# Loading k, b and v of the first three chunks in eight-step rows in a fused recurrence and feed-forward kernel

## The chip, the cores and the metric

The kernel runs on one core of one Trainium2 chip. The metric is the device time of one execution in microseconds (us), and less is better. A profile shows one execution with its engines: PE multiplies matrices and turns (transposes) tiles, with PEld its weight loads; DVE, ACT and POOL work element by element; SP issues most DMAs. PE writes to PSUM, here four slots of two banks each, and DVE and ACT read it from there.

## The reference

A recurrence over 768 steps for 4 batches of 8 heads with 40 features, and then a feed-forward layer on its output. `state` is a 40 by 40 matrix for each of the 32 heads:

```python
for t in range(S):
    y[:, :, t] = np.einsum('bhd,bhde->bhe', rt, state)
    Sa = np.einsum('bhde,bhe->bhd', state, at)
    state_decay = state * wt[:, :, None, :] - np.einsum('bhd,bhe->bhde', Sa, bt)
    state = state_decay + np.einsum('bhd,bhe->bhde', vt, kt)
...
x = attn_out.transpose(0, 2, 1, 3).reshape(B * S, H * D)      # 3072 x 320
h = x @ w_in                                                   # 320 x 2048
r = np.maximum(h, 0.0)
return ((r * r) @ w_out).astype(np.float32)                    # 2048 x 320
```

All inputs and the output are float32; the kernel multiplies in bfloat16.

## The kernel before

The 768 steps are cut into 12 chunks (`NCH`) of 64 steps. Within a chunk the recurrence is written as matrix products, and only the state goes from chunk to chunk. Partitions hold 64 steps twice: half `g` holds the 16 heads of two batches.

`load(c)` issues the DMAs of a chunk on SP. w, k, b and v are loaded "steps first": one partition for each step, and in it a run of 40 numbers (160 bytes) for each of 16 heads. a and r are loaded "in eight-step rows": eight steps of one head stand together in DRAM, so that one run has 320 numbers (1,280 bytes); partitions are then pairs of heads and groups of eight steps.

`prep(c)` makes the factors of a chunk. `ln` takes logarithms of w; `hi` and `lo` split them into two bfloat16 parts; `ci` sums them over the steps by a triangular matrix, and `ei` and `ex` take exp of minus and plus the sum (`iG`, `Gin`); `cf` makes the same sums turned, features on the partitions, and `ef` their exp (`GT`). `mulKB` (two halves) multiplies the loaded k and b by `iG` into `KB`, steps first. `TK` turns `KB` on PE and `tK` copies it to `KBT`, features first. `castA`, `TA`, `tA` and `castR`, `TR`, `tR` bring a and r features first (`AR`); `castV` copies v into one half of `VU`. The products `EN` of `KBT` and `AR` are masked by `mEN` into a triangle.

`rec(c)` is the recurrence: `AS` (state times a) and `EV` (triangle times v) add up in one PSUM slot, `u0` copies it, `NU` adds the second order term, and `u1` writes u beside v into `VU`. `SC` and `S` make the new state, `s` scales it, and `TS` and `tS` turn it. So the chain from chunk to chunk goes AS, EV, u0, NU, u1, S, s.

`read(c)` makes the output: `TV` turns the whole of `VU` and `tV` copies it to `VUT`; `CX` and `mCX` are the second triangle; `RS` and `Y` give the output, `y` and `yd` scale it, and `XT` and `xt` turn it. `ffn(c)` is the feed-forward layer of 256 rows: for each quarter `u`, `F` and `FL` multiply by the first matrix, `f` cuts at zero, `q` squares, and `O` multiplies by the second matrix; `o` copies the result out and `st` stores it.

`weights()` loads the matrices in pieces into buffers that other work uses later, and casts them: `lwl` and `cwl` (the last 64 rows of the first matrix), `lwi` and `cwi` (its four quarters of 256 rows), `lwo` and `cwo` (eight pieces of the second). The quarters use two buffers in turn, so a load of a quarter waits for the cast of the quarter two before it. Chunks 0 to 3 (`WHOLE`) are turned by 128 by 128 transposes, the later ones by narrower ones, two at a time.

The order of all this is written out in the string `ORDER`, some 1,000 entries such as `PE0 TK 0` or `POOL castV 0 g1`: an engine (for PE the PSUM slot too) and a step. Each engine runs its entries strictly in that order; the waits between engines follow from the data. SP's queue is such a list too: a DMA that waits for its buffer holds back all DMAs behind it. Every PE step is recorded at line 385 (products), 389 (narrow turns) or 392 (wide turns), and copies at 366 (DVE), 371 (ACT) and 375 (POOL), so that steps are told apart by their tiles.

## Time and profile before

| | |
|---|---|
| Median of three runs | 254.06 us |
| The runs | 254.0, 254.06 and 254.92 us |
| Profiled execution, first to last instruction (the only time that its profile gives) | 254.1 us |
| Busy: PE, DVE, ACT, POOL | 225.3, 180.6, 161.0, 150.5 us |
| Mean granted PE clock | 0.962 of full speed |
| Moved by DMA | 33.55 MB in 114,089 packets, 101,238 of them under 512 bytes |

The profiled execution is one run and its span stands within 0.1 us of the median. Busy times of different engines overlap. "Idle before" in a profile line is the time for which an engine had nothing to run ahead of that instruction, with what ended it. A PE that is busy is not always at its full clock: the column of the granted clock tells.

### The profile page before, as it was taken

The page shows a single profiled execution, that of the slowest core. Times are in us where ns is not written, and L with a number is a line of the kernel's source. Part 1 is how long each engine was busy: PE and PEld are TensorE (multiplying, and loading weights), DVE is VectorE, ACT ScalarE, POOL GpSimd, SP SyncE. Part 2 cuts the span into 40 slices and gives each one's busy share as a digit, 9 for nine tenths or more (in the row PEclk, how much of TensorE's full clock was granted, in tenths as well). Part 3 has the DMA queues.
Part 4 walks back from the last instruction along what each step waited for, and adds up shares of the span by engine and source line. Part 5 has one row for each costly group of instructions (what it writes and reads, how often), then busy time and mean ns, then how long its engine had stood idle before and what let it go on. Part 6 is the DMA issues. An engine that isn't in the chain of part 4 may idle for free.

```text
span 254.1 us, 12021 instructions
## 1 busy us (share of the span) xinstructions
PE 225.3 (89%) x5472; PEld 176.3 (69%) x5472; DVE 180.6 (71%) x216; ACT 161.0 (63%) x233; POOL 150.5 (59%) x128
## 2 busy tenths in 40 slices
PE   0547768999888999998999989999999999999991
PEld 0436757777776877776777777767777787878870
DVE  7463895987976976887659877799566779667301
ACT  3435676678955889773677657776578563762920
POOL 3581710695874688198688563998459950320860
PEclk9975697999999999999999999999999999999998
DMA  6999897888888986885586988798570020202021
GB/s 133 181 212 164 182 238 159 188 157 215 207 138 202 193 162 135 172 153 113 114 159 173 201 143 161 141 165 167 112 142 19 4 57 3 57 3 54 0 50 56
DMA packets 114089, 33.55 MB, mean 132 GB/s; under 512 B 101238, under 2 KB 113014, under 8 KB 114038
## 3 DMA queue, kind: packets, MB, share of 16 engines
q1 hardware_dynamic: 113894, 32.62, 64.1%
q8 instruction: 43, 0.70, 1.2%
q10 hardware_dynamic: 144, 0.16, 0.2%
q14 instruction: 8, 0.07, 0.1%
...
## 4 chain that ended last, share of the span: by engine, by line
PE 58%; DMA 12%; SPq 8%; ACT 7%; DVE 7%; issue 4%; POOL 3%; ACTq 0%; POOLq 0%; DVEq 0%
PE pb L385 49%; PE pb L389 5%; DMA raw_w<-in_w_dram 4%; PE pb L392 4%; SPq L411 2%; SPq L404 2%; DMA osb<-in_moe_w_out_dram 2%; POOL KB L379 2%; DVE EN L605 2%; DMA raw_r<-in_r_dram 2%; DMA raw_kb<-in_b_dram 2%; SPq L435 1%; DMA raw_kb<-in_k_dram 1%; SPq L425 1%; ACT iG L493 1%
## 5 line engine op out<-in xcount | busy, mean ns | idle before, releaser
L852 POOL TENSOR_TENSOR G<-G 128x1024 bf16<-128x1024 bf16 x37 | 69.4, 1891 | 37.5 <-ACT G L844 37.3
L385 PE MATMUL pb<-WOUT,G 128*128 128x320 bf16 x384 | 57.3, 300 | 1.0 <-ACT WOUT L371 0.9
L385 PE MATMUL pb<-XT,WIN 128*128 128x256 bf16 x384 | 48.8, 274 | 0.0
L844 ACT ACTIVATE G<-pb 128x1024 bf16<-128x1024 f32 x37 | 37.4, 1024 | 14.7 <-PE pb L385 14.6
L385 PEld LDWEIGHTS <-G 128*128 128x128 bf16 x384 | 35.4, 98 | 15.2 <-issue 1.7
L379 POOL TENSOR_TENSOR KB<-raw_kb,iG 128x640 bf16<-128x640 f32 x20 | 30.6, 1542 | 24.3 <-DMA raw_kb<-in_b_dram 14.6
L385 PEld LDWEIGHTS <-WIN 128*128 128x128 bf16 x384 | 34.7, 98 | 8.3 <-issue 3.7
L605 DVE TENSOR_TENSOR CX<-pb,MSKI 128x1024 bf16<-128x1024 f32 x24 | 29.1, 1219 | 5.2 <-PE pb L385 4.6
L605 DVE TENSOR_TENSOR EN<-pb,MSK 128x1024 bf16<-128x1024 f32 x24 | 29.0, 1221 | 4.8 <-PE pb L385 3.7
L499 ACT ACTIVATE Gin<-pb 64x320 f32<-64x320 f32 x48 | 20.3, 428 | 6.3 <-PE pb L385 5.8
L580 DVE TENSOR_TENSOR AR<-pb,GT 128x512 bf16<-128x512 bf16 x24 | 15.7, 683 | 10.1 <-PE pb L392 4.2
L697 DVE TENSOR_TENSOR STb<-pb,GT 64x640 bf16<-64x640 f32 x22 | 18.0, 819 | 5.8 <-PE pb L385 5.5
L371 ACT ACTIVATE VU<-pb 64x640 bf16<-64x640 f32 x24 | 16.7, 697 | 7.4 <-PE pb L385 7.1
L493 ACT ACTIVATE iG<-pb 128x640 f32<-128x640 f32 x24 | 16.7, 698 | 6.3 <-PE pb L385 4.7
L775 DVE TENSOR_TENSOR Yb<-pb,Gin 128x128 bf16<-128x128 f32 (+1 forms) x24 | 12.4, 550 | 11.4 <-PE pb L385 11.4
L385 PEld LDWEIGHTS <-EN 64*64 64x64 bf16 x768 | 15.0, 113 | 6.2 <-issue 3.2
L379 POOL TENSOR_TENSOR lo<-lnW,hi 128x640 bf16<-128x640 f32 x12 | 16.8, 1398 | 3.8 <-issue 3.2
L366 DVE COPY KBT<-pb 128x2048 bf16<-128x2048 bf16 x12 | 14.6, 1219 | 5.7 <-PE pb L389 3.5
L371 ACT ACTIVATE osb<-pb 128x640 f32<-128x640 f32 (+1 forms) x13 | 8.4, 644 | 15.4 <-PE pb L385 14.9
L375 POOL CAST VU<-raw_v 64x640 bf16<-64x640 f32 x20 | 15.2, 761 | 4.8 <-DMA raw_v<-in_v_dram 4.2
L846 DVE TENSOR_SCALAR G<-pb 128x1024 bf16<-128x1024 f32 x11 | 13.4, 1220 | 5.2 <-PE pb L385 4.7
L385 PE MATMUL pb<-XT,WLAST 64*128 64x256 bf16 x192 | 16.4, 271 | 0.2 <-DVE CX L605 0.2
...
## 6 DMA issues: line engine op xcount, KB each, us to landing
...
```

The source lines that it names most:

```text
L366: lambda: nc.vector.tensor_copy(out=o_(), in_=i_())))
L371: alts.append(("ACT", c_act(n), lambda: nc.scalar.activation(out=o_(), in_=i_(), func=ACTF.Copy, scale=1.0 if scale is None else scale)))
L375: lambda: nc.gpsimd.tensor_copy(out=o_(), in_=i_())))
L379: return [("POOL", 40 + 2.35 * n, lambda: nc.gpsimd.tensor_tensor(out=o_(), in0=a_(), in1=b_(), op=op)), ("DVE", c_dve(n), lambda: nc.vect ...
L385: return lambda: nc.tensor.matmul(out=o_(), lhsT=l_(), rhs=r_(), start=start, stop=stop, skip_group_check=True)
L493: ew(f"ei {c} h{jh}", [("ACT", c_act(2 * n), lambda hb=hb, jh=jh: nc.scalar.activation(out=iG[0][:].rearrange("p (g j) e -> p g (j e)", g= ...
L499: nc.scalar.activation(out=Gin[c % NGI][rows(g), NP * jh:NP * jh + NP, :].rearrange("p j e -> p (j e)"), in_=slot(hb, FP32)[rows(g), g, 0: ...
L580: ew(f"tA {c} g{g}", [("DVE", c_dve(512), lambda g=g: nc.vector.tensor_tensor(out=steps(AR[q2][:, 0, g]), in0=turned(ha, g), in1=steps(GT[ ...
L605: evac(f"m{nm} {c} g{g}", lambda s, n: [("DVE", c_dve(n), lambda: nc.vector.tensor_tensor(out=dst[q2][:, g, s].rearrange("p q i t -> p (q ...
L697: ew(f"s {c} q{q}", [("DVE", c_dve(2 * n), lambda q=q: nc.vector.tensor_tensor(out=STb[q2][rows(q), :, q, 0:D], in0=slot(hs, FP32)[rows(q) ...
L844: ("ACT", c_act(1024), lambda gb=gb, hf=hf: nc.scalar.activation(out=gb, in_=slot(hf, FP32)[:], func=ACTF.Relu)),
L852: ("POOL", 1900, lambda gv=gv: nc.gpsimd.tensor_tensor(out=gv, in0=gv, in1=gv, op=ALU.mult)),
```

## The change

Chunks 0 to 2 (`RUNS` for k and b, `VRUNS` for v) get a path of their own.

- k, b and v of these chunks are loaded in eight-step rows, runs of 1,280 bytes in place of 160.
- `turned_kb` takes the place of `ei`, `mulKB`, `TK` and `tK`. It casts k and b to bfloat16 (`castK`, `castB`), turns them (`TK`, 32 narrow transposes), multiplies by exp of minus the turned sums (`eg`, from the slot of `cf`) in `tK`, two halves, and turns the product back (`BK`, 16 wide transposes) to fill `KB` (`bK`).
- `turned_v` takes the place of `castV` and of the v half of `TV`: `castV`, 16 narrow transposes (`VT`), two copies into `VUT` (`vt`), 16 transposes back (`BV`) and two copies into `VU` (`bV`).
- `turned_u` turns the u half alone: `UT`, and two copies (`ut`).
- Each quarter of the first matrix is loaded by two DMAs with runs of 1,024 bytes in place of one with 2,048.
- There are three more small buffers (`tKB` twice, `tV`), which are cleared at the start.
- `ORDER` is new throughout, for the steps of all chunks. Its beginning, up to the first state:

```
SP ldw 0; SP ldb 0; SP ldw 1; SP ldk 0; ACT ln 0; POOL hi 0; SP ldv 0; POOL lo 0; SP lda 0; POOL
castB 0; PE0 ci 0 h1; PE1 cf 0; SP ldw 2; ACT ex 0 h1 g1; ACT ln 1; DVE castK 0; PE2 TK 0; ACT eg
0; SP ldv 1; DVE castV 0; ACT ex 0 h1 g0; PE3 VT 0; DVE tK 0 g1; ACT ef 0; PE0 ci 0 h0; POOL castA
0; SP ldk 1; ACT vt 0 g0; DVE tK 0 g0; PE1 TA 0; ACT ex 0 h0 g1; SP ldb 1; ACT hi 1; DVE tA 0 g0;
PE2 BK 0; ACT vt 0 g1; DVE tA 0 g1; SP lda 1; ACT ex 0 h0 g0; PE3 BV 0; ACT castV 1; DVE lo 1; ACT
bK 0; PE1 VT 1; SP ldr 0; POOL castK 1; PE0 cf 1; DVE vt 1 g0; ACT ef 1; DVE bV 0 g0; PE2 EN 0 g0;
SP lwl 0; DVE bV 0 g1; DVE mEN 0 g0; ACT vt 1 g1; PE3 EN 0 g1; POOL castB 1; ACT eg 1; SP ldr 1;
DVE mEN 0 g1; PE1 TK 1; ACT ln 2; POOL castA 1; PE0 ci 1 h1; SP ldb 2; PE2 ci 1 h0; DVE tK 1 g0;
PE3 EV 0; ACT ex 1 h0 g1; POOL castR 0; ACT ex 1 h0 g0; SP lda 2; ACT ex 1 h1 g0; POOL hi 2; PE2
TR 0; DVE tK 1 g1; ACT ex 1 h1 g1; ACT u0 0; POOL lo 2; PE0 TA 1; SP lwi 0 u0; ACT tR 0 g1; PE NU
0; DVE tA 1 g1; ACT cwl 0; PE1 BK 1; DVE tA 1 g0; DVE u1 0 g0; PE0 EN 1 g0; DVE tR 0 g0; ACT u1 0
g1; SP lwi 0 u1; DVE bK 1; PE2 EN 1 g1; PE3 ci 2 h1; DVE mEN 1 g1; ACT ex 2 h1 g0; PE1 UT 0; SP
ldw 3; ACT ex 2 h1 g1; ACT ut 0 g0; PE3 S 0 g0; DVE mEN 1 g0; PE2 ci 2 h0; ACT ut 0 g1; ACT ex 2
h0 g0; PE1 CX 0 g0; ACT castA 2; DVE mCX 0 g0; PE0 BV 1; ACT castR 1; PE S 0 g1; ACT bV 1 g1; DVE
s 0 q0; PE1 cf 2; SP ldk 2; ACT ex 2 h0 g1; DVE s 0 q1; ...
```

The code, without the new `ORDER`:

```diff
+    RUNS = range(3)
+    VRUNS = range(3)
...
+    tKB = buf("tKB", [128, 8, 2, 64], BF16, 2)
+    tV = buf("tV", [128, 8, 2, 64], BF16, 1)
...
+    def runs_of(c, y):
+        return raw_kb[c % NKBR][:].rearrange("p h e -> p (h e)")[:, 640 * y:640 * y + 640].rearrange(
+            "p (q x) -> p q x", q=2)
...
-        for nm, x in (("k", k), ("b", b)):
+        for y, (nm, x) in enumerate((("k", k), ("b", b))):
+            def go_runs(y=y, x=x):
+                xv = x[:, :, t0, :].rearrange("b (p q) (k i) e -> q (b p) k (i e)", q=2, i=8)
+                for q in range(2):
+                    nc.sync.dma_start(out=runs_of(c, y)[:, q, :], in_=xv[q])
+            if c in RUNS:
+                plan.add(f"ld{nm} {c}", [("SP", 1100)], ("ew", {"SP": go_runs}),
+                         writes=[("raw", nm, c % NKBR)])
+                continue
...
+        def go_v_runs():
+            xv = v[:, :, t0, :].rearrange("b (p q) (k i) e -> q (b p) k (i e)", q=2, i=8)
+            to = raw_v[c % NV][:].rearrange("p (q i) e -> p q (i e)", q=2)
+            for q in range(2):
+                nc.sync.dma_start(out=to[:, q, :], in_=xv[q])
+        plan.add(f"ldv {c}", [("SP", 1100 if c in VRUNS else 2400)],
+                 ("ew", {"SP": go_v_runs if c in VRUNS else go_v}), writes=[("raw", "v", c % NV)])
...
+    def turned_v(c):
+        q2 = c % 2
+        ew(f"castV {c}", copy_alts(
+            lambda: tV[0][:, :, :, 0:D].rearrange("p i q e -> p q i e"),
+            lambda: raw_v[c % NV][:].rearrange("p (q i) e -> p q i e", q=2), 640, True,
+            engines=("POOL", "ACT", "DVE")),
+           reads=[("raw", "v", c % NV)], writes=[("tV",)])
+        hb = ("A", "VT", c)
+        ms = [tp(lambda i=i, g=g: slot(hb, BF16)[:, g, 0:512].rearrange(
+                     "p (m i k) -> p m i k", i=8, k=8)[:, :, i, :],
+                 lambda i=i, g=g: tV[0][rows(g), i].rearrange("p q e -> p (q e)"), g)
+              for i in range(8) for g in range(2)]
+        pe(f"VT {c}", "R", 64, ms, reads=[("tV",)], writes=[hb], alloc=[hb])
+        for g in range(2):
+            ew(f"vt {c} g{g}", copy_alts(
+                lambda g=g: VUT[q2][:, NP * g:NP * g + NP, 1 - g, :].rearrange(
+                    "p m (k i) -> p m k i", i=8),
+                lambda g=g: slot(hb, BF16)[:, g, 0:512].rearrange("p (m i k) -> p m k i", i=8, k=8),
+                512),
+               reads=[hb], writes=[("VUT", q2, f"s{g}")], free=[hb])
+        ht = ("A", "BV", c)
+        ms = [tpw(lambda m=m, g=g: slot(ht, BF16)[rows(1 - g), 0, 128 * m:128 * m + 128],
+                  lambda m=m, g=g: VUT[q2][:, NP * g + m, 1 - g, :])
+              for m in range(NP) for g in range(2)]
+        pe(f"BV {c}", "C", 128, ms, reads=both(("VUT", q2)), writes=[ht], alloc=[ht])
+        for g in range(2):
+            ew(f"bV {c} g{g}", copy_alts(
+                lambda g=g: VU[c % NK][rows(1 - g), NJ * g:NJ * g + NJ, 0:D],
+                lambda g=g: slot(ht, BF16)[rows(1 - g), 0].rearrange("p (j e) -> p j e", e=64)[:, :, 0:D],
+                640, True),
+               reads=[ht], writes=[("VU0", c % NK, g)], free=[ht])
+
+    def turned_u(c, VU1):
+        q2 = c % 2
+        hb = ("A", "UT", c)
+        ms = [tp(lambda m=m, g=g: slot(hb, BF16)[:, g, 64 * m:64 * m + 64],
+                 lambda m=m, g=g: VU[c % NK][rows(g), NJ * g + 2 * m:NJ * g + 2 * m + 2, :].rearrange(
+                     "p h e -> p (h e)"), g)
+              for m in range(NP) for g in range(2)]
+        pe(f"UT {c}", "R", 64, ms, reads=VU1, writes=[hb], alloc=[hb])
+        for g in range(2):
+            ew(f"ut {c} g{g}", copy_alts(
+                lambda g=g: VUT[q2][:, NP * g:NP * g + NP, g, :],
+                lambda g=g: slot(hb, BF16)[:, g, 0:512].rearrange("p (m t) -> p m t", t=64), 512),
+               reads=[hb], writes=[("VUT", q2, f"s{g}", "u")], free=[hb])
+
+    def turned_kb(c, hf, KBK):
+        q2 = c % 2
+        iGT = iG[0][:].rearrange("p h e -> p (h e)")[:, 0:NJ * L].rearrange("p (m t) -> p m t", t=L)
+        ew(f"eg {c}", [("ACT", c_act(1024), lambda: nc.scalar.activation(
+            out=iGT.rearrange("p (g m) t -> p g m t", g=2),
+            in_=slot(hf, FP32)[:].rearrange("p g (m t) -> p g m t", t=L), func=ACTF.Exp, scale=-1.0))],
+           reads=[hf], writes=[("iG", 0), ("iG", 1)], free=[hf])
+        for y, nm in enumerate("kb"):
+            ew(f"cast{nm.upper()} {c}", copy_alts(
+                lambda y=y: tKB[y][:, :, :, 0:D].rearrange("p i q e -> p q i e"),
+                lambda y=y: runs_of(c, y).rearrange("p q (i e) -> p q i e", e=D), 640, True,
+                engines=("POOL", "ACT", "DVE")),
+               reads=[("raw", nm, c % NKBR), ("left", "k", c % NKBR), ("left", "b", c % NKBR)],
+               writes=[("tKB", y)])
+        hb = ("A", "TK", c)
+        ms = []
+        for i in range(8):
+            for y in range(2):
+                for g in range(2):
+                    ms.append(tp(
+                        lambda i=i, y=y, g=g: slot(hb, BF16)[
+                            :, g, 512 * (y ^ 1 ^ g):512 * (y ^ 1 ^ g) + 512].rearrange(
+                            "p (m i k) -> p m i k", i=8, k=8)[:, :, i, :],
+                        lambda i=i, y=y, g=g: tKB[y][rows(g), i].rearrange("p q e -> p (q e)"), g))
+        pe(f"TK {c}", "R", 64, ms, reads=[("tKB", 0), ("tKB", 1)], writes=[hb], alloc=[hb])
+        for g in range(2):
+            gm = slice(NP * g, NP * g + NP)
+            ew(f"tK {c} g{g}", [("DVE", c_dve(1024), lambda g=g, gm=gm: nc.vector.tensor_tensor(
+                out=KBT[q2][:, gm].rearrange("p m x (k i) -> p x m k i", i=8),
+                in0=slot(hb, BF16)[:, g].rearrange("p (x m i k) -> p x m k i", x=2, i=8, k=8),
+                in1=iGT[:, gm].rearrange("p (o m) (k i) -> p o m k i", o=1, i=8).broadcast_to(
+                    [128, 2, NP, 8, 8]), op=ALU.mult))],
+               reads=[hb, ("iG", 0), ("iG", 1)], writes=[("KBT", q2, f"s{g}")], free=[hb])
+        ht = ("A", "BK", c)
+        ms = [tpw(lambda pi=pi: pairs_at(ht, pi),
+                  lambda pi=pi: KBT[q2][:, pi].rearrange("p x t -> p (x t)")) for pi in range(NJ)]
+        pe(f"BK {c}", "D", 128, ms, reads=both(("KBT", q2)), writes=[ht], alloc=[ht])
+        ew(f"bK {c}", copy_alts(
+            lambda: KB[c % NK][:].rearrange("p (m q) e -> p m q e", q=2)[:, :, :, 0:D],
+            lambda: slot(ht, BF16)[:].rearrange("p h (m q e) -> p (h m) q e", q=2, e=64)[:, :, :, 0:D],
+            1280, True),
+           reads=[ht], writes=KBK, free=[ht])
...
+            if c not in RUNS:
+                ew(f"ei {c} h{jh}", [("ACT", c_act(2 * n), lambda hb=hb, jh=jh: nc.scalar.activation(
...
+        if c in RUNS:
+            turned_kb(c, hf, KBK)
+        for jh in range(0 if c in RUNS else 2):
...
+        if c in VRUNS:
+            turned_v(c)
+        for g in range(0 if c in VRUNS else 2):
...
-            triangle("EN", EN, KBT, 0, MSK, c, g, both(("KBT", q2)) + [("AR", q2, g)])
+            triangle("EN", EN, KBT, 0, MSK, c, g,
+                     ([("KBT", q2, f"s{g}")] if c in RUNS else both(("KBT", q2))) + [("AR", q2, g)])
...
+        if c in VRUNS:
+            turned_u(c, VU1)
+        else:
...
-            triangle("CX", CX, VUT, 1, MSKI, c, g, both(("VUT", q2)) + [("RR", q2, g)])
+            triangle("CX", CX, VUT, 1, MSKI, c, g, both(("VUT", q2)) + [("RR", q2, g)]
+                     + ([("VUT", q2, f"s{g}", "u")] if c in VRUNS else []))
...
-            plan.add(f"lwi 0 u{u}", [("SP", 1700)], ("ew", {"SP": lambda u=u, i=i:
-                     nc.sync.dma_start(out=stage(i).rearrange("p (k x) -> p k x", k=2),
-                                       in_=wi[u])}), writes=held(i))
+
+            def quarter(u=u, i=i):
+                for x in range(2):
+                    cols = slice(256 * x, 256 * x + 256)
+                    nc.sync.dma_start(out=stage(i).rearrange("p (k x) -> p k x", k=2)[:, :, cols],
+                                      in_=wi[u][:, :, cols])
+            plan.add(f"lwi 0 u{u}", [("SP", 1700)], ("ew", {"SP": quarter}), writes=held(i))
```

322 lines of the change are left out of this document (154 added, 168 removed).

## The prediction

> **What bounds the kernel now.** I read the page first, then busy time by stretches, then the chain and the waits of the first 60 us, and last the durations by shape.
>
> ```profile
> span 254.1 us, 12021 instructions
> PE 225.3 (89%) x5472; PEld 176.3 (69%) x5472; DVE 180.6 (71%) x216; ACT 161.0 (63%) x233; POOL 150.5 (59%) x128
> DMA  6999897888888986885586988798570020202021
> ```
> ```profile
> 0.00:10.00 10.00, 1.19 (x8) 0.68 (x10) 7.71 (x20) 2.76 (x3) 5.26 (x18) 1.00 0.76 152
> 10.00:20.00 10.00, 5.78 (x103) 4.47 (x99) 5.10 (x6) 4.92 (x9) 6.48 (x6) 0.82 1.23 199
> 20.00:30.00 10.00, 8.17 (x165) 7.32 (x166) 4.91 (x8) 7.07 (x12) 3.79 (x4) 0.50 0.81 155
> 30.00:40.00 10.00, 6.71 (x237) 5.36 (x237) 8.58 (x9) 5.71 (x9) 2.62 (x4) 1.00 0.99 219
> 58.00:100.00 42.00, 39.28 (x992) 30.84 (x986) 32.98 (x37) 32.83 (x52) 29.89 (x26) 1.00 0.84 179
> 150.00:240.00 90.00, 89.70 (x2252) 70.38 (x2247) 66.82 (x75) 56.89 (x79) 52.68 (x38) 1.00 0.42 81
> 240.00:254.10 14.10, 8.65 (x64) 6.00 (x62) 1.00 (x3) 3.28 (x5) 5.42 (x3) 0.92 0.18 48
> ```
>
> Columns: window, length, busy PE, PEld, DVE, ACT, POOL, then granted clock, DMA share, GB/s. PE is the bound: of its 28.8 us of idleness (254.1 less 225.3), 18.2 lie before 40 us (10 less each busy figure), 5.4 in the tail, 2.7 between 58 and 100, and 0.3 in the 90 us from 150. So the change, which sits in chunks 0 to 2, can win in the head and in the waits that loads leave behind it. DMA is busy throughout to about 190 us.
>
> ```profile
> POOL KB L379 <- DMA raw_kb<-in_b_dram: 14.6, 2, 11.9
> ```
> ```profile
> 20.51 1.04 PE L385 MATMUL pb<-VU,EN 64*64 64x40 bf16 x31 [0.89 <-DVE EN L605]
> 35.78 0.68 PE L385 MATMUL pb<-VU,EN 64*64 64x40 bf16 x32
> 57.70 0.68 PE L385 MATMUL pb<-VU,EN 64*64 64x40 bf16 x32
> 22.98 1.04 PE L385 MATMUL pb<-NZ,EN 64*64 64x40 bf16 x32
> 27.35 1.89 PE L392 MATMUL pb<-IDQ,VU 128*128 128x128 bf16 x16
> 44.71 1.07 PE L392 MATMUL pb<-IDQ,VU 128*128 128x128 bf16 x16
> 5.60 0.74 ACT L471 ACTIVATE lnW<-raw_w 128x640 f32<-128x640 f32 x1 [3.52 <-DMA raw_w<-in_w_dram]
> 6.47 0.72 POOL L375 CAST hi<-lnW 128x640 bf16<-128x640 f32 x1 [3.26 <-ACT lnW L471]
> 7.82 1.39 POOL L379 TENSOR_TENSOR lo<-lnW,hi 128x640 bf16<-128x640 f32 x1
> 7.13 2.12 DVE L942 COPY IDQ<-IDb 64x64 bf16<-64x64 bf16 x2
> ```
>
> The first three rows are EV 0, EV 1 and EV 2, one per chunk: my milestones (20.5, 35.8, 57.7). Chunk 2 comes 22 us after chunk 1, and POOL waited 11.9 us for b of chunk 2: there the head is bound by loads. The rows below show one group of 32 at half clock (1.04) and at full (0.68), and 16 wide transposes so (1.89, 1.07).
>
> **The change, part by part.** *Loads.* Nine loads (k, b, v of three chunks) of 2 x 160 KB go from 160-byte to 1,280-byte runs.
>
> ```profile
> 4.60:6.60 2.00, 0.00 (x0) 0.00 (x0) 1.67 (x3) 0.74 (x1) 0.12 (x1) 1.00 0.94 277
> 9.00:13.00 4.00, 3.40 (x53) 2.88 (x53) 0.87 (x2) 2.70 (x5) 1.31 (x2) 1.00 1.15 170
> 14.60:16.60 2.00, 1.07 (x16) 0.90 (x16) 0.49 (x1) 0.94 (x2) 1.66 (x3) 0.93 1.08 219
> 31.00:34.00 3.00, 1.50 (x83) 1.29 (x83) 2.49 (x4) 2.05 (x4) 1.61 (x3) 1.00 0.97 296
> ```
>
> By SP's order these are stretches of a and r (1,280 bytes, 277 GB/s), of rows (160 bytes, 170), of lwl (1,024 bytes, 219), and of the first matrix with r (2,048 bytes, 296). Nine loads are 2.95 MB: 17.3 us at 170, 10.6 at 277, 6.7 saved. The matrix (2.10 MB) goes from 7.1 us at 296 to 9.6 at 219: 2.5 lost. Net 4.2 us less transfer.
>
> When do they land? Up to k 2, SP's new order carries four w (1.31 MB at 170 GB/s, 7.7 us), 13 loads in long runs (4.26 MB at 277, 15.4), lwl and half the matrix (1.57 MB at 219, 7.2): 30.3 us, and 3 us from first issue to first landing (w landed 5.5 us in, its own 1.9 us of transfer taken off) make 34 us. Six more loads bring b 3 at about 43. castK 2 wants k 2 at about 37, mulKB 3 wants b 3 at 43 at the earliest. Two waits are new in SP's queue: lwi 0 u1 waits for cwl 0 on ACT, with w 3, k 2, v 2 and w 4 behind it, and lwi 0 u2 for cwi 0 u0 on POOL, with a 3, lwi 0 u3 and k 4 behind it. By my walk SP reaches the first about when cwl 0 ends (24 us), and what is behind the second is wanted after 48 us. So I cost both at nothing; without that cover each costs about one load, 1.2 to 1.9 us. The Trainium skill (DMA: Bandwidth & Descriptors, Specifications) gives 512 bytes as the smallest run for full rate; by it the matrix edit costs 0 instead of 2.5. The 219 against 296 speaks against that, and as these loads end under cover, neither figure enters the end.
>
> *Engine work.*
>
> ```profile
> L366 DVE COPY KBT<-pb 128x2048 bf16<-128x2048 bf16 x12 | 14.6, 1219 | 5.7 <-PE pb L389 3.5 <-PE pb L392 2.2
> L605 DVE TENSOR_TENSOR EN<-pb,MSK 128x1024 bf16<-128x1024 f32 x24 | 29.0, 1221 | 4.8 <-PE pb L385 3.7 <-POOL lo L379 0.8
> L580 DVE TENSOR_TENSOR AR<-pb,GT 128x512 bf16<-128x512 bf16 x24 | 15.7, 683 | 10.1 <-PE pb L392 4.2 <-ACT GT L515 3.1 <-PE pb L389 1.8
> L697 DVE TENSOR_TENSOR STb<-pb,GT 64x640 bf16<-64x640 f32 x22 | 18.0, 819 | 5.8 <-PE pb L385 5.5
> L366 DVE COPY Sb<-pb 128x1280 bf16<-128x1280 bf16 x8 | 6.6, 819 | 0.8 <-PE pb L389 0.7
> L775 DVE TENSOR_TENSOR Yb<-pb,Gin 128x128 bf16<-128x128 f32 x12 | 3.4, 284 | 6.7 <-PE pb L385 6.7
> L366 DVE COPY XT<-pb 128x768 bf16<-128x768 bf16 x12 | 6.6, 554 | 4.7 <-PE pb L389 4.5
> L366 DVE CAST WOUT<-osb 128x640 bf16<-128x640 f32 x1 | 0.5, 485 | 0.0
> L381 DVE TENSOR_TENSOR KB<-raw_kb,iG 128x640 bf16<-128x640 f32 x4 | 5.7, 1420 | 0.8 <-ACT iG L493 0.8
> L371 ACT ACTIVATE AR<-pb 128x512 bf16<-128x512 bf16 x18 | 10.2, 594 | 6.3 <-PE pb L389 5.2 <-PE pb L392 0.8 <-DVE AR L366 0.3
> L371 ACT ACTIVATE VU<-pb 64x640 bf16<-64x640 f32 x24 | 16.7, 697 | 7.4 <-PE pb L385 7.1
> L515 ACT ACTIVATE GT<-pb 128x1024 f32<-128x1024 f32 x12 | 12.3, 1023 | 3.9 <-DVE STb L697 2.4 <-PE pb L385 1.3
> L385 PE MATMUL pb<-XT,WIN 128*128 128x256 bf16 x384 | 48.8, 274 | 0.0
> L385 PE MATMUL pb<-XT,WLAST 64*128 64x256 bf16 x192 | 16.4, 271 | 0.2 <-DVE CX L605 0.2
> ```
>
> Gone per chunk: two mulKB, two castV, two ei, one wide TK and TV, and one tK and one tV of 1.22. Added: eg (as GT, 1.02), three casts (0.49 on DVE), two tK that now multiply (twice the 0.68 of 512 columns is 1.37, a row of 1,024 gives 1.22; I take 1.22), bK (0.82), two vt and two ut (0.59 on ACT, taken as 0.69 like tA on DVE), two bV (0.48 to 0.70). DVE, ACT and POOL together get 2 to 3 us more per chunk, PE about 0.6 (two wide sets become one wide, four narrow and BV). Three more clearings of buffers (tKB, tV) on DVE end before k 0 lands. POOL takes over all four cwi and gives up six mulKB; it had 2.62 of 10 us busy between 30 and 40, which covers them.
>
> *The new order of chunks 3 to 11* moves steps everywhere, and no row prices that. It can win at most the idleness that is there, 2.7 us between 58 and 100, 0.3 from 150 on, and 2.2 in the rest (28.8 less 18.2, 5.4, 2.7 and 0.3); a new wait of 0.5 us in each of nine chunks would lose 4.5. I take a gain of 1.3, explained below.
>
> *To EV 0.* castA 0 leaves its place before lo 0, so lo 0 runs 7.1 to 8.5; ci (0.5, an estimate: half a group) and cf (a group of 32, 1.04) end about 10.2, eg at 11.3. DVE's queue to the mask of EN 0 is then two tK 2.44, two tA 1.37, lo 1 0.82, vt 0.69, two bV 0.96, two mEN 2.44: 8.7, that is 20.0, and about 0.9 of waiting behind castV 1 and BV 0: EV 0 at 20.9. Nothing won.
>
> *To the new state of chunk 0.* PE is next, at half clock: EV 1.04, TR and TA 0.95 each, NU 1.04, BK 1 1.89, six groups of 16 at 0.52 (EN 1 twice, UT 0, S 0 twice, CX 0), two ci at 0.5, BV 1 0.95: 10.9, so s 0 starts about 31.8.
>
> *To EV 1.* DVE: two s 1.64, mCX 1.22, castB 2 0.49, tS 0.82: 36.0 for u0 1, against EV 1 at 35.8 to 36.5 before. Still nothing won, but k and b of chunk 2 have landed.
>
> *To EV 2.* DVE: u0 0.82, yd and y 1.10 (0.28, and 640 columns like s), two tA 1.37, two tK 2.44, xt 0.55, two mCX 2.44, two s 1.64, bV 0.48, mEN 1.22, y and yd 1.10, mulKB 3 1.42, mEN 1.22: 15.8, so EV 2 at 51.8 against 57.7. This is the gain: 5.9 us.
>
> *To the end.* Before, 196.4 us follow EV 2 (254.1 less 57.7). The new order has then done three F and FL groups fewer (F 0 u2, u3, F 1 u1): 48.8/48 plus 16.4/48 is 1.36 each, 4.1. It still owes BK 2 (1.07) and TR 2 (0.54), has TK 3 (1.07) and ci 3 h0 (0.3) behind it, and UT 2 for TV 2 saves 0.5: together 3.8. 51.8 + 196.4 + 3.8 = 252.0. Of the 2.7 us idle between 58 and 100 the earlier loads and stored F groups take back between nothing and all; I take half, 1.3: **250.7 us**. The tail stays: its last products, evictions and stores are the same. The span and the median of the runs (254.06) agree, so nothing is added.
>
> **Rivals.**
>
> ```profile
> 18.11 2.35 DVE L605 TENSOR_TENSOR EN<-pb,MSK 128x1024 bf16<-128x1024 f32 x2 [0.78 <-POOL lo L379]
> ```
>
> *More is won.* If PE gets the full clock at about 23 us, leg two is bound by DVE and 1.6 us shorter, EV 2 loses the small overlaps of consecutive DVE instructions (two mEN take 2.35, not 2.44; some 1 us over the leg), and all 2.7 us of idleness go: 250.7 - 1.6 - 1.0 - 1.4 = 246.7. For it: PE is nearly unbroken from 18 us on in my walk, while before it was at half clock with 8.17 of 10 busy. Against: PE and DVE must both run without a gap. The Trainium skill (TensorE: Matmul & The Clock Gate, What's actually happening) has full clock follow one busy window of about 3.4 us; the half clock over 20 to 30 us at 82% busy shows that "busy" must be nearly gapless.
>
> *It evens out.* DVE and ACT stall on each other for 2 to 4 us in the last leg: EV 2 at 55 gives 254.
>
> *Slower: the half clock lasts.* From 32 us to EV 2 PE has about 18 us of groups (24 of about 0.5, four wide sets of 1.07, two F with FL of 1.36), and DVE 20. At full clock PE just keeps pace. If the clock stays half to 44 us, 12 us bring 6 us of work and the other 12 follow: EV 2 at 56 plus 2 of stalls gives 256.9. It decides from about 5 us of loss on. For: PE waits in between; against: 30 to 40 us before ran at 1.00 with 6.71 busy.
>
> *Slower: DVE and POOL block each other.* The tiny IDQ copies took 2.12 us for two beside POOL, mulKB on DVE a mean of 1.42. castK, castV, lo 1, castB 2 and mulKB 3 h0 move to DVE; at 1 us each plus POOL's share: 256.5. My walk has POOL idle beside most of them. The Trainium skill (SBUF — State Buffer, Who interferes with whom) makes it an exclusive lock, the later one stopped until the first ends; the trace agrees, as the copies end at 9.25 (7.13 + 2.12) and POOL's lo at 9.21.
>
> **How the numbers follow.** Forecast (248.5 to 252.8) 0.45; more won 0.17; evened out 0.14; half clock 0.14; blocking 0.10. About 0.5% (1.3 us) is what a measurement can tell from no change: faster 0.62, same 0.14, slower 0.24. Range 246.5 to 257.0, which leaves out about half of the case of more won and less than half of the two slower ones, under 0.2 together; the forecast's own is 248.5 to 252.8.
>
> **What would show it.** Right: EV 0 and EV 1 near 21 and 36, EV 2 near 52; POOL's 11.9 us wait gone; DVE over 9 of 10 busy from 32 to 52; a tail of 5.4 idle. Wrong: PE clock 0.50 beyond 35 us, EV 2 after 55, or new PE idleness after 150 us, where it has 0.3.

## The result and the profile after

The changed kernel is a little faster than the kernel before: by 0.6%, where I had forecast 1.3%. It was timed three times, each time beside the kernel before on the same chip. The ratios and all counts of executions below leave a few disturbed executions out.

| | changed, median | before, median | ratio (95% interval) |
|---|---|---|---|
| first timing | 253.54 us | 254.93 us | 0.9946 (0.9925 to 0.9967) |
| second | 252.11 us | 253.92 us | 0.9914 (0.9878 to 0.9949) |
| third | 251.57 us | 253.88 us | 0.9928 (0.9894 to 0.9962) |

Weighted by their intervals they give 0.9936, within 0.0016: a gain of 1.6 us in 254. One timing's interval is some 0.3% (0.8 us) to either side, so that half a microsecond between two runs is not told from none in what follows. The kernel before, timed once against itself, gave 0.9969 (0.9935 to 1.0004): it takes the three timings together to carry a gain of 0.6%.

The page of the changed kernel, the same three lines as before:

```profile
span 252.5 us, 12415 instructions
PE 227.0 (90%) x5664; PEld 178.9 (71%) x5664; DVE 193.9 (77%) x244; ACT 180.7 (72%) x246; POOL 113.0 (45%) x105
DMA  5989968899989798878775868446762010004003
```

PE has 1.7 us more to do and idles 25.5 us instead of 28.8. The busy times by stretches, with the columns as in the prediction:

```profile
0.00:10.00 10.00, 1.76 (x36) 1.25 (x36) 6.24 (x21) 2.90 (x4) 5.31 (x18) 1.00 0.76 165
10.00:20.00 10.00, 7.96 (x172) 6.76 (x173) 7.84 (x13) 8.36 (x14) 2.17 (x3) 1.00 0.85 214
20.00:30.00 10.00, 7.14 (x208) 5.69 (x208) 9.38 (x11) 8.13 (x15) 3.51 (x4) 0.96 0.97 254
30.00:40.00 10.00, 8.97 (x282) 7.85 (x281) 8.95 (x13) 8.46 (x14) 4.32 (x5) 0.86 0.84 183
58.00:100.00 42.00, 40.53 (x994) 31.58 (x990) 34.55 (x39) 35.32 (x46) 22.30 (x20) 1.00 0.90 185
150.00:240.00 90.00, 89.33 (x2210) 70.15 (x2207) 69.92 (x82) 63.29 (x79) 31.48 (x23) 1.00 0.34 73
240.00:252.50 12.50, 7.27 (x54) 5.00 (x52) 2.70 (x5) 0.61 (x2) 3.69 (x2) 0.95 0.19 52
```

PE's idleness before 40 us is 14.2 us (18.2 before), between 58 and 100 1.5 (2.7), from 150 to 240 0.7 (0.3), in the tail 5.2 (5.4). The milestones EV 0, EV 1 and EV 2, and a wait that was not there before:

```profile
21.77 0.68 PE L392 MATMUL pb<-VU,EN 64*64 64x40 bf16 x32
35.32 0.68 PE L392 MATMUL pb<-VU,EN 64*64 64x40 bf16 x32
53.15 0.68 PE L392 MATMUL pb<-VU,EN 64*64 64x40 bf16 x32
...
56.87 1.05 PE L392 MATMUL pb<-XT,WIN 128*128 128x256 bf16 x8 [1.10 <-POOL WIN L382]
```

EV 0 and EV 1 stand where the prediction put them (21 and 36), EV 2 1.4 us later than its 51.8. The last row is F 0 u3, which waits 1.1 us for the cast of the last quarter of the first matrix. POOL had waited 2.0 us for that quarter's load, and its wait for b (11.9 before) is 7.8, now for b of chunk 3:

```profile
POOL KB L386 <- DMA raw_kb<-in_b_dram: 7.8, 1, 7.8
POOL WIN L382 <- DMA G<-in_moe_w_in_dram: 2.4, 2, 2.0
```

DVE is the bound ahead of EV 2, as forecast:

```profile
32.00:52.00 20.00, 19.04 (x24) 0.98 0.84 191
```

(DVE alone, from 32 to 52 us: 19.0 of 20 busy.) That holds up to the last mask; what follows it up to EV 2 is PE's own work, as the part on the prediction shows. From these two profiles the shortfall seemed plain: EV 2 1.4 us late, and a wait of 1.1 us that I had priced at nothing. Both turned out to be traits of single executions.

### The profile page after: what moved, and what is told of

It reads as the page before. It is cut to its first block, busy times and chain, and to the rows that moved or that the text cites. A ratio compares the mean times of both kernels' runs of the same rounds, so it can differ in the third digit from the quotient of the medians.

```text
span 252.5 us, 12415 instructions
## 1 busy us (share of the span) xinstructions
PE 227.0 (90%) x5664; PEld 178.9 (71%) x5664; DVE 193.9 (77%) x244; ACT 180.7 (72%) x246; POOL 113.0 (45%) x105
## 4 chain that ended last, share of the span: by engine, by line
PE 66%; DVE 8%; ACT 8%; SPq 6%; DMA 5%; issue 2%; POOL 2%; POOLq 0%; ACTq 0%
PE pb L392 57%; PE pb L396 6%; DMA G<-in_moe_w_in_dram 3%; PE pb L399 2%; ACT G L969 2%; ACT Gin L614 2%; DMA raw_w<-in_w_dram 1%; SPq L423 1%; DVE STb L818 1%; SPq L431 1%; DVE EN L726 1%; DMA raw_a<-in_a_dram 1%; ACT AR L378 1%; DVE CX L726 1%; POOL WIN L382 1%
## 5 line engine op out<-in xcount | busy, mean ns | idle before, releaser
L977 POOL TENSOR_TENSOR G<-G 128x1024 bf16<-128x1024 bf16 x23 | 43.8, 1919 | 45.4 <-ACT G L969 38.9
L392 PE MATMUL pb<-WOUT,G 128*128 128x320 bf16 x384 | 57.3, 300 | 0.4 <-ACT VU L378 0.2
L386 POOL TENSOR_TENSOR KB<-raw_kb,iG 128x640 bf16<-128x640 f32 x13 | 19.9, 1543 | 32.6 <-ACT iG L608 18.0
L971 DVE TENSOR_SCALAR G<-pb 128x1024 bf16<-128x1024 f32 x13 | 15.8, 1219 | 3.7 <-PE pb L392 3.6
L378 ACT ACTIVATE osb<-pb 128x640 f32<-128x640 f32 (+1 forms) x10 | 6.2, 622 | 16.7 <-PE pb L392 16.3
L386 POOL TENSOR_TENSOR lo<-lnW,hi 128x640 bf16<-128x640 f32 x9 | 13.1, 1451 | 10.7 <-ACT hi L378 10.4
L630 ACT ACTIVATE GT<-pb 128x1024 f32<-128x1024 f32 x12 | 12.3, 1022 | 7.0 <-PE pb L392 6.9
L979 ACT ACTIVATE G<-G 128x1024 bf16<-128x1024 bf16 x16 | 16.4, 1050 | 0.1
L378 ACT ACTIVATE VU<-pb 64x640 bf16<-64x640 f32 (+1 forms) x20 | 13.9, 697 | 2.4 <-PE pb L392 1.4
L608 ACT ACTIVATE iG<-pb 128x640 f32<-128x640 f32 x18 | 12.6, 698 | 3.9 <-PE pb L392 3.5
L392 PE MATMUL pb<-hi,UTI 64*128 64x320 bf16 x48 | 7.8, 320 | 7.9 <-POOL hi L382 7.1
```

The lines of the kernel that those rows point to most:

```text
L378: alts.append(("ACT", c_act(n), lambda: nc.scalar.activation(out=o_(), in_=i_(), func=ACTF.Copy, scale=1.0 if scale is None else scale)))
L386: return [("POOL", 40 + 2.35 * n, lambda: nc.gpsimd.tensor_tensor(out=o_(), in0=a_(), in1=b_(), op=op)), ("DVE", c_dve(n), lambda: nc.vect ...
L392: return lambda: nc.tensor.matmul(out=o_(), lhsT=l_(), rhs=r_(), start=start, stop=stop, skip_group_check=True)
L971: ("DVE", c_dve(1024), lambda gb=gb, hf=hf: nc.vector.tensor_scalar(out=gb, in0=slot(hf, FP32)[:], scalar1=0.0, scalar2=None, op0=ALU.max))],
L977: ("POOL", 1900, lambda gv=gv: nc.gpsimd.tensor_tensor(out=gv, in0=gv, in1=gv, op=ALU.mult)),
L979: ("ACT", c_act(1024), lambda gv=gv: nc.scalar.activation(out=gv, in_=gv, func=ACTF.Square))],
```

## The experiments

Ratios are to the kernel before, timed beside each run; the changed kernel itself stands at 0.9936.

**The first matrix: shape of its runs, and place in SP's queue.** One DMA with 2,048-byte runs for each quarter again:

```diff
-                for x in range(2):
-                    cols = slice(256 * x, 256 * x + 256)
-                    nc.sync.dma_start(out=stage(i).rearrange("p (k x) -> p k x", k=2)[:, :, cols],
-                                      in_=wi[u][:, :, cols])
+                nc.sync.dma_start(out=stage(i).rearrange("p (k x) -> p k x", k=2), in_=wi[u])
```

> The changed kernel, with each quarter of the first matrix loaded by one DMA in 2,048-byte runs again. After the change PE waits 1.1 us for the last quarter's cast (at 56.87 us), and the quarters land a median of 5.6 us after their issue. If the short runs are what makes the last quarter late (2.5 us more transfer over four quarters, worked out from 219 against 296 GB/s), that wait goes and the end comes 0.5 to 1.5 us earlier, near 252.5. If the order in SP's queue makes it late, the issue times hardly move, the wait shrinks by under 0.5 us, and the time stays within 0.5 us of the changed kernel's.

0.9953 (0.992 to 0.9986): nothing that can be told; the wait for the cast was 0.8 us. The form of these loads does not matter to the end, as I had said of it. Then the order:

```diff
- SP lwo 0 x1; SP ldk 3; SP lwo 0 x0; SP ldb 3; SP lwi 0 u2; SP lda 3; SP lwi 0 u3; SP ldk 4
- POOL cwi 0 u2; POOL cwo 0 x1; POOL cwi 0 u3
+ SP lwo 0 x0; SP ldk 3; SP ldb 3; SP lwi 0 u2; SP lwi 0 u3; SP lda 3; SP lwo 0 x1; SP ldk 4
+ POOL cwi 0 u2; POOL cwi 0 u3; POOL cwo 0 x1
```

> The changed kernel, with the last two quarters of the first matrix ahead of a 3, of k 4 and of two pieces of the second matrix in SP's queue, and POOL's cast of one piece moved behind the cast of the last quarter; 1,024-byte runs kept. Theory of the late matrix: the wait of 1.1 us at 56.87 us and the 2.0 us that POOL waits for the same load go, F 0 u3 starts 1 us earlier and the end comes 0.7 to 1.5 us earlier. Rival, PE-bound by its extra turning: PE has 1.7 us more to do than before, so F 0 u3 starts earlier but the idleness comes back elsewhere before 100 us, and the time stays within 0.4 us.

0.9892 (0.9848 to 0.9936), and in its profile the wait was gone. That looked like a find. With the edit to SP's queue alone:

```diff
- POOL cwi 0 u2; POOL cwi 0 u3; POOL cwo 0 x1
+ POOL cwi 0 u2; POOL cwo 0 x1; POOL cwi 0 u3
```

> The run with the last quarters of the matrix earlier in SP's queue, but with POOL's cast of a piece of the second matrix left ahead of the cast of the last quarter, as in the changed kernel. If SP's order makes the gain of that run (1.4 us from the changed kernel), it stays, within 0.5 us: 0.988 to 0.991 of the kernel before. If POOL's order does (it waits for that piece, whose load now comes later), F 0 u3 waits again and the time goes back to 0.993 to 0.995.

0.9925 (0.9882 to 0.9968), with 1.0 us of waiting at that place again: undecided between the two. So it and the changed kernel were timed side by side:

> The changed kernel beside the run with the matrix earlier in SP's queue, on one chip: 0.991 to 0.995 of the kernel before, as in its two timings so far (0.9946 and 0.9914).

> The run with the last quarters of the matrix earlier in SP's queue, once more (0.9892 the first time). In later profiles of the changed kernel PE waited 0.3 us for the last quarter, not 1.1. If the late matrix was a trait of that one execution, this run now stands within 0.3% of the changed kernel beside it; if the queue's order is worth 1.4 us, it is 0.5% below it again.

0.9928 and 0.9917: 251.57 us against 251.72. The mended queue is worth nothing that can be measured. The wait itself is a trait of single executions. PE's waits between 40 and 58 us in the second profile of the changed kernel:

```profile
PE pb L392 <- DVE XT L373: 0.4, 1, 0.4
PE pb L392 <- ACT iG L608: 0.3, 1, 0.3
PE pb L392 <- ACT VU L378: 0.3, 1, 0.3
PE pb L392 <- POOL WIN L382: 0.3, 1, 0.3
```

The same wait is 0.3 us here. The theory of the late matrix falls.

**EV 2 earlier.** In the last leg DVE spends 1.80 us on mulKB 3 h0 ahead of the mask for which EV 2 waits (in the other four profiles of the changed kernel it takes 0.82 to 1.50):

```profile
49.32 1.80 DVE L388 TENSOR_TENSOR KB<-raw_kb,iG 128x640 bf16<-128x640 f32 x1
```

```diff
- PE0 TK 3; PE2 AS 2; PE3 XT 1; PE EV 2           (DVE mulKB 3 h0 before mEN 2 g1, tK 3 after)
+ PE3 AS 2; PE EV 2; PE0 TK 3; PE2 XT 1           (DVE mEN 2 g1; mulKB 3 h0; tK 3)
```

> The changed kernel with the state of chunk 2 taken first: on PE, AS 2 ahead of TK 3 and XT 1 and TK 3 behind EV 2; on DVE, mulKB 3 h0 and tK 3 behind the second mask of EN 2 (the slots 2 and 3 trade names from there on). In the changed kernel's profile mulKB 3 h0 took 1.80 us on DVE ahead of that mask, so EV 2 should come 1.8 to 2.5 us earlier, near 51. Theory that my rule was right (the end moves as EV 2 does, less the PE work put behind it, 1.07 for TK 3 and 0.51 for XT 1): the end comes 0.5 to 1.0 us earlier. Theory of the late matrix: F 0 u3 waits for its quarter until 56.9 us as before, the idleness grows there by what EV 2 gained, and the time stays within 0.4 us.

The same together with the two edits above to the queues of SP and POOL:

> The run with the last quarters of the matrix earlier in SP's queue, with the state of chunk 2 taken first as well. That run stood at 0.9892 of the kernel before, with EV 2 still at 53.2. If the matrix hid what an earlier EV 2 is worth, this adds 0.5 to 1.0 us to it: 0.985 to 0.987 of the kernel before. If PE is bound by its work by then, nothing is added: 0.988 to 0.990.

And that with its new waits mended:

```diff
- ACT f 0 u0; ACT ef 3           - DVE tK 3; DVE tS 1        - ACT bK 2; ACT xt 1
+ ACT ef 3; ACT f 0 u0           + DVE tS 1; DVE tK 3        + ACT xt 1; ACT bK 2
- PE0 BK 2; PE1 FL 0 u3; PE NU 2; PE F 0 u3     - DVE lo 4; DVE u1 2 g0
+ PE NU 2; PE1 FL 0 u3; PE F 0 u3; PE0 BK 2     + DVE u1 2 g0; DVE lo 4
```

> The run with both edits (matrix earlier in SP's queue, state of chunk 2 first), with the waits mended that it showed between 48 and 58 us: on ACT ef 3 ahead of f 0 u0 (PE waited 0.8 us for it before AS 2), on DVE tS 1 ahead of tK 3, on PE NU 2, FL 0 u3 and F 0 u3 ahead of BK 2 (which waited 1.0 us for tK 3), on ACT xt 1 ahead of bK 2. Its EV 2 was at 50.8 and PE idled 2.7 us between 40 and 58. If the rest of the gain went into these waits, 1.0 to 1.8 us come back: 0.985 to 0.988 of the kernel before. If PE's idleness only moves on, it stays at 0.990 to 0.992.

EV 2 came at 51.5, 50.8 and 50.1 us; the ratios are 0.9915 (0.9884 to 0.9945), 0.9913 (0.9881 to 0.9946) and 0.9942 (0.9911 to 0.9972). None differs from the changed kernel's. PE alone up to EV 2 and from there on, in the run with both edits and in the one with the waits mended as well:

```profile
0.00:50.78 50.78, 34.48 (x986) 1.00 0.89 213
50.78:249.90 199.12, 190.48 (x4683) 1.00 0.55 114
```

```profile
0.00:50.10 50.10, 34.67 (x986) 1.00 0.86 210
50.10:251.30 201.20, 190.52 (x4682) 1.00 0.55 115
```

What EV 2 gains comes back behind it, as work put there (190.5 us of PE work instead of 189.3, the mean of the changed kernel's profiles below) or as idleness (199.12 less 190.48 is 8.6, and 10.7 in the other). EV 2 is 0.6, 1.3 and 2.0 us ahead of the changed kernel's mean of 52.1, and 1.0 to 1.2 us of work went behind it. So there was 0.8 us to win at most, and one timing does not tell that from none: whether the end still follows an EV 2 near 52 us, these runs do not show.

**Is PE's extra turning what eats the gain?** In the changed kernel's profile, the turning of one chunk (TK, VT, BV, BK and UT of chunk 2):

```profile
38.38 0.64 PE L396 MATMUL pb<-IDb,tKB 64*128 64x64 bf16 x32
42.22 0.41 PE L396 MATMUL pb<-IDb,tV 64*128 64x64 bf16 x16
45.46 0.64 PE L399 MATMUL pb<-IDQ,VUT 128*64 128x128 bf16 x16
53.77 1.07 PE L399 MATMUL pb<-IDQ,KBT 128*128 128x128 bf16 x16
61.16 0.41 PE L396 MATMUL pb<-IDb,VU 64*128 64x64 bf16 x16
```

That is 3.17 us against two wide sets of 1.07: 1.03 more per chunk, not the 0.6 of my estimate. Doubling BK and BV:

```diff
-        pe(f"BK {c}", "D", 128, ms, reads=...
+        pe(f"BK {c}", "D", 128, ms * 2, reads=...
-        pe(f"BV {c}", "C", 128, ms, reads=...
+        pe(f"BV {c}", "C", 128, ms * 2, reads=...
```

> The changed kernel with the transposes back (BK and BV) of chunks 0 to 2 done twice over, to the same result: by the profile 1.07 and 0.64 us each at full clock, 5.1 us more for PE in the head in all. If the extra turning is hidden behind DVE there, as I thought, the end moves by 0 to 1.5 us. If PE has no slack in the head and its extra turning ate the gain, it moves by 4 to 5 us, near 257.

1.0048 (1.0012 to 1.0083), 0.011 above the changed kernel: 2.8 us for 5.1 us of work. Its eleven executions spread from 253.1 to 257.6 us; their plain median, 256.4, would make it 4.0 us, and the profiled one has a span 4.4 us over the changed kernel's mean. So PE's work in the head is hidden in part only, by a fifth to a little under half, neither free nor fully paid. In the changed kernel this price lies in its EV 2 already.

**What are the loads worth?** First all nine in short runs under the new order:

```diff
-                for q in range(2):
-                    nc.sync.dma_start(out=runs_of(c, y)[:, q, :], in_=xv[q])
+                for g in range(2):
+                    nc.sync.dma_start(out=raw_kb[c % NKBR][rows(g)].rearrange("p h e -> p (h e)")[
+                        :, 640 * y:640 * y + 640].rearrange("p (h e) -> p h e", e=D), in_=half(x, g))
...
-                 ("ew", {"SP": go_v_runs if c in VRUNS else go_v}), ...
+                 ("ew", {"SP": go_v}), ...
```

> The changed kernel, its k, b and v of chunks 0 to 2 loaded in 160-byte runs into the same buffers at the same places of the queue. (These rows are then steps first, so that the values of these chunks are misplaced; the instructions are the same.) My prediction priced this load saving at 6.7 us of transfer and all of the gain at EV 2 (the triangle's product of chunk 2). If so, EV 2 goes from 53.2 to 57 or later and the end comes 4 to 6 us later, 257 to 260. If the new order of the steps makes the gain and the loads are hidden, EV 2 and the end move by less than 1.5 us.

1.0259 (1.0214 to 1.0305), 8.2 us over the changed kernel. EV 2 of this run:

```profile
61.19 0.68 PE L392 MATMUL pb<-VU,EN 64*64 64x40 bf16 x32
```

It is 9 us late, and the end with it: here the loads bind. They bind early: EV 0 stands at 27.4, 5.6 us late already. PE's list has VT 1 and TK 1 ahead of EV 0, and for their loads ACT waits 2.2 us (v 1), POOL 5.8 (k 1) and 2.2 (b 1). Then v alone:

```diff
-    VRUNS = range(3)
+    VRUNS = range(0)
...
- DVE castV 0; ACT castV 1; POOL castV 2; PE VT, BV, UT and ACT or DVE vt, bV, ut of chunks 0 to 2
+ POOL castV 0 g1; POOL castV 0 g0; ACT castV 1 g1; ACT castV 1 g0; POOL castV 2 g1; POOL castV 2 g0
+ PE TV 0 to 2 and ACT tV 0 to 2 at the places of UT and the first ut
```

> The changed kernel with v of chunks 0 to 2 as before: loaded in 160-byte runs and cast into VU, VU turned whole (TV, tV), and no VT, vt, BV, bV, UT, ut. By the profile PE has 0.39 us less per chunk (TV's 1.07 against VT 0.41, BV 0.64, UT 0.41), 1.2 in all, and the loads have 2.2 us more of transfer (0.98 MB at 170 against 277 GB/s). If PE's extra turning is what ate the gain, half of 1.2 comes back (0.4 to 0.8 us earlier); if the load time is still worth what it is with all nine loads short (8 us for nine, so 2.6 for three), the end comes 1.5 to 3 us later.

1.0119 (1.0071 to 1.0166), 4.6 us later, EV 2 at 56.7: more than my 1.5 to 3. This run says less than I wanted, since I had put the copy of all of VUT on ACT, and PE waited for it:

```profile
PE pb L387 <- ACT VUT L373: 2.6, 2, 1.3
```

And the long runs alone, in the kernel before:

```diff
             def go(nm=nm, x=x, y=y):
+                if c < 3:
+                    xv = x[:, :, t0, :].rearrange("b (p q) (k i) e -> q (b p) k (i e)", q=2, i=8)
+                    to = raw_kb[c % NKBR][:].rearrange("p h e -> p (h e)")[
+                        :, 640 * y:640 * y + 640].rearrange("p (q x) -> p q x", q=2)
+                    for q in range(2):
+                        nc.sync.dma_start(out=to[:, q, :], in_=xv[q])
+                    return
```

(and the same for v)

> The kernel before, its k, b and v of chunks 0 to 2 loaded in 1,280-byte runs into the same buffers, with its old order and engine work. (The rows are then eight-step rows where the kernel takes steps first, so that the values of these chunks are misplaced.) If the loads bound its head, as its 11.9 us wait of POOL for b of chunk 2 says, EV 2 comes 3 to 6 us earlier than 57.7 and the end 2 to 5 us earlier, 249 to 252. If PE, at half clock, and the engines' work bound it as much, EV 2 moves by under 2 us and the end by under 1.5 us.

0.9928 (0.9897 to 0.9959): 1.8 us, as much as the whole change. EV 2 of this run:

```profile
56.33 0.68 PE L385 MATMUL pb<-VU,EN 64*64 64x40 bf16 x32
```

That is 0.9 us before the mean of the kernel before (57.2, below), though POOL no longer waits for b of chunk 2: EV 2 did what the second theory said, and the end came out just past its 1.5 us. So POOL's wait of 11.9 us was not what held EV 2 back. PE had other work meanwhile, in the kernel before from 40 to 58 us:

```profile
40.00:58.00 18.00, 17.72 (x376) 0.91 0.80 178
```

The four kernels together: the long runs are worth 1.8 us in the old order and 8.2 in the new. With long runs, the turning, which is what makes rows so loaded usable, and the new order around it bring EV 2 4 us earlier and move the end by nothing that can be measured (0.9936 against 0.9928); with short runs they cost 6.6 us (1.0259).

**Was the base of the sum sound?** Each run's time is longer than its span: by a median of 1.74 us for the kernel before and 1.93 for the changed one. In the 96 executions of the kernel before whose span is on record, the median span is 252.1 us, and only three reach the 254.1 of the profile from which I worked. Hence further profiles of both kernels, unedited:

> The kernel before, profiled once more. All runs so far take 1.8 to 2.0 us longer than their span from first to last instruction, and 37 runs of the kernel before have a median span of 252.3 us; the profile from which I worked has 254.1. So my sum may have started from an execution some 1.8 us longer than most. If so, this profile has a span of 251.5 to 253 and fewer us of PE idleness or a higher clock in the head than 18.4 idle before 58 us and 0.50 between 20 and 30, and a part of the gain that I forecast was never there to win. If that profile was typical, this one has 253.5 or more.

> The changed kernel, timed and profiled once more, as the basis of the comparisons with the experiments run beside it: 0.9946 of the kernel before again, within 0.3%; the wait of PE for the last quarter of the matrix (1.1 us at 56.9) is there again, and POOL's 2.0 before it.

> The kernel before, a third profile. Its first had 18.4 us of PE idleness up to EV 2 and 10.4 after it, its second 17.7 and 8.3 (span 250.8). If the sum started from an execution in which late loads of later chunks added 2 us, this one has 17.5 to 18.5 up to EV 2 and 8 to 9.5 after it. If the second was the odd one, it has over 10 after it again.

> The kernel before, a fourth profile, for the same: by the theory of the odd first execution, 8 to 9.5 us of PE idleness after EV 2 and a span of 250.5 to 252.5; by its rival over 10 and over 253.

> The changed kernel, a third profile. Its first two had EV 2 at 53.2 and 51.6, 15.7 us of PE idleness up to it both times, 9.8 and 9.0 after it, and spans of 252.5 and 250.2. If my forecast of the changed kernel held in span and only its base was off: EV 2 at 51.5 to 53.2, a span of 250 to 252.5, idleness after EV 2 of 8.5 to 10.

> The changed kernel, a fourth profile, for the same: EV 2 at 51.5 to 53.2 and a span of 250 to 252.5; work on PE after EV 2 of 189.5 us, as in the two before.

The second profile of the kernel before came out at 250.8 us, shorter than either theory had it; the third has 9.6 us of idleness after EV 2, just over the 9.5, and the fourth 8.1 and a span of 251.2, as the theory of the odd first execution says. Of the changed kernel, the second timing missed the 0.3% narrowly (0.9914), and the wait at 56.9 was 0.3 us in place of 1.1. Its third profile was below all three of its ranges (51.4, 248.3 and 7.7), its fourth inside them.

PE alone up to EV 2 and from there to the end, in the first and the second profile of the kernel before:

```profile
0.00:57.70 57.70, 39.27 (x856) 0.85 0.90 181
57.70:254.10 196.40, 186.05 (x4620) 0.99 0.58 118
```

```profile
0.00:56.92 56.92, 39.20 (x857) 1.00 0.94 184
56.92:250.80 193.88, 185.63 (x4620) 1.00 0.58 119
```

and in the first and the third of the changed kernel:

```profile
0.00:53.15 53.15, 37.46 (x1008) 0.97 0.87 202
53.15:252.50 199.35, 189.52 (x4658) 1.00 0.57 114
```

```profile
0.00:51.43 51.43, 35.65 (x1009) 1.00 0.88 212
51.43:248.30 196.87, 189.21 (x4658) 0.99 0.56 115
```

The difference of length and busy time is PE's idleness. From these rows and the same rows of the other profiles (four of before, five of the changed kernel with the one timed side by side above):

| | before: each | mean | changed: each | mean |
|---|---|---|---|---|
| EV 2 | 57.7, 56.9, 56.9, 57.3 | 57.2 | 53.2, 51.6, 51.4, 51.8, 52.7 | 52.1 |
| PE work after EV 2 | 186.1, 185.6, 186.0, 185.8 | 185.9 | 189.5, 189.6, 189.2, 189.3, 188.8 | 189.3 |
| idle after EV 2 | 10.4, 8.3, 9.6, 8.1 | 9.1 | 9.8, 9.0, 7.7, 9.0, 7.3 | 8.6 |
| span | 254.1, 250.8, 252.5, 251.2 | 252.2 | 252.5, 250.2, 248.3, 250.1, 248.9 | 250.0 |

Span is the sum of the first three, within rounding. The work after EV 2 repeats within 0.8 us; it is EV 2 and the idleness behind it that differ from one execution to the next. In the first execution of the kernel before, PE's waits between 58 and 150 us begin so:

```profile
PE pb L385 <- ACT WOUT L371: 0.9, 1, 0.9
PE pb L385 <- ACT osb L371: 0.9, 1, 0.9
PE pb L389 <- ACT G L844: 0.8, 1, 0.8
PE pb L392 <- POOL WOUT L375: 0.6, 1, 0.6
```

and in the second:

```profile
PE pb L385 <- ACT WOUT L371: 0.9, 1, 0.9
PE pb L392 <- POOL WOUT L375: 0.6, 1, 0.6
```

The two waits of 0.9 and 0.8 us for ACT, in chunks that the change does not load otherwise, are missing there. That late loads of w hold ACT up at those places (ACT waits 4.3 us for w between 100 and 150 us in the first profile, 1.1 in the second) fits, but the third has 2.3 us of that wait with no such idleness on PE, so this cause stays open.

## Why the prediction was wrong

Near in number were the marks of the sum. EV 0, forecast at 20.9, has a mean of 21.8 in five executions, EV 2, at 51.8, one of 52.1. The work moved behind it, forecast at 3.8 us, is 3.4 (189.3 less 185.9). The span forecast for the changed kernel was 250.7 us; 39 executions have a median of 250.5.

For EV 2 that is luck: two errors of the walk cancel. The walk kept PE at half clock until s 0 at 31.8 us and found "Still nothing won" at EV 1. PE was at full speed by 20 us in four of the five profiles (the second half of EN 0 took 0.41 us there, and 0.61 in the fifth), and EV 1 came at 35.3, 34.0, 33.9, 34.2 and 35.2 (mean 34.5; before 35.8, 36.8, 35.9 and 37.1, mean 36.4): 1.9 us were won by then. The leg from there was forecast at 15.8 us and took 17.6 to 17.8 in all five. DVE's share of it is right: from the start of u0 1 to the end of the last mask it took 15.3 to 16.1 us. But EV 1 starts some 0.8 us before u0 1, and the walk let EV 2 start as that mask ends, where PE's list has TK 3, AS 2 and XT 1 first. In the second profile the mask ended at 50.18, and PE went on without a gap:

```profile
49.73 1.05 PE L399 MATMUL pb<-IDQ,KB 128*128 128x128 bf16 x16
50.72 0.48 PE L392 MATMUL pb<-STb,AR 128*64 128x80 bf16 x16
51.12 0.51 PE L399 MATMUL pb<-IDQ,Yb 128*128 128x128 bf16 x6
51.56 0.68 PE L392 MATMUL pb<-VU,EN 64*64 64x40 bf16 x32
```

EV 2 starts 0.9 to 1.5 us after that mask in the five.

Wrong was also "there the head is bound by loads", said of the stretch before EV 2: with the loads early and the old order, EV 2 came at 56.3, and in the kernel before PE was busy for 17.7 of the 18 us from 40 to 58. What the change did win lies earlier. A span is PE's work and its idleness; in the means PE's idleness up to 40 us falls from 17.4 to 14.3, from there to EV 2 it rises from 0.6 to 1.2, behind EV 2 it falls from 9.1 to 8.6, and PE has 0.9 us more work (225.0 to 225.9).

The number failed at the sentence that joined the sum to the measured time: "The span and the median of the runs (254.06) agree, so nothing is added." They agree by accident. A span of 254.1 belongs to a run of about 255.8 us (254.1 + 1.74, an estimate: that run's own time is not on record), and the runs' median of 254.06 to a span of about 252.3. Two errors of equal size cancel in that line. They do not cancel in the forecast: 250.7 was a span, and as a time it is 250.7 + 1.93 = 252.6 us, close to the 252.4 that is the median of the changed kernel's 39 executions. And the gain was counted from an execution 2.0 us longer than the median one (254.1 less 252.1): of the forecast 3.4 us, 1.4 remain against a usual execution, and 1.6 were measured. These medians join three timings that differ: the changed kernel's are 251.6, 250.1 and 249.7 us in span. In the first timing both kernels ran longer; its 18 executions of the kernel before, the three of my base among them, have a median of 254.93 us, where all the later ones have 253.9 to 254.1. So about half of the 2.0 us may lie in that session and not in the one execution, and the forecast meets each timing only within 1 us.

In the means of the profiles the sum reads 5.1 (EV 2) less 3.4 (work) plus 0.5 (idleness), 2.2 us, where I had 5.9 less 3.8 plus 1.3. Of the 0.8 at EV 2, 0.5 is the odd base (57.7 for a mean of 57.2). The idleness was mis-sized, and the odd execution is a part of that too. I let the changed kernel win back 1.3 us of idleness behind EV 2. In the means it wins 0.5 (9.1 to 8.6). Between 58 and 100 us it does win 1.6 (3.0 to 1.4), but it pays 0.4 between EV 2 and 58 (0 before), 0.2 from 100 to 150 (0.7 to 0.9) and 0.6 from 150 to 240 (0.1 to 0.7); the tail gives 0.1. The 0.6 is the new PE idleness after 150 us that I had named as a sign of error; it is there in all five profiles.

Of the rivals, the one in which more is won saw half of its mechanism come true: EV 0 took 0.68 us in four of five profiles, where it took 1.04 before. In the first and the fifth PE fell back to half clock for some 3 us at 30 us (0.50 granted from 30 to 32). BV 1 in the first profile and in the second:

```profile
30.69 1.07 PE L399 MATMUL pb<-IDQ,VUT 128*64 128x128 bf16 x16
```

```profile
29.57 0.64 PE L399 MATMUL pb<-IDQ,VUT 128*64 128x128 bf16 x16
```

These are the two with EV 1 at 35.3 and 35.2 and EV 2 at 53.2 and 52.7; in the other three they come 1.2 and 1.4 us earlier in the mean. So the relapse accounts for the late EV 2 of the first profile. The spans do not follow it (252.5 and 248.9 with it, 248.3 to 250.2 without). The rival of a half clock that lasts beyond 35 us fell with that. Blocking between DVE and POOL was seen, at the size of one instruction (mulKB 3 h0 took 1.80 us beside a POOL cast of 1.31, and 0.82 in the third profile). It did not set EV 2: the leg from EV 1 took 17.6 to 17.8 us with all of these.

The waits in SP's queue, priced at nothing, are worth nothing that these runs can tell: three timings with the quarters earlier (0.9892, 0.9925, 0.9917) overlap the changed kernel's own three, and side by side 0.15 us parted them. The runs of 1,024 bytes against 2,048, at whose price the Trainium skill (DMA: Bandwidth & Descriptors, Specifications; 512 bytes suffice for full rate) and the row of 219 GB/s differed, do not enter the end, as forecast; these runs measure the end alone, so they leave the rate itself undecided.
